# Reordering VectorE's work in a gated mix of two state-space layers: spectral products, the inverse transform, and scans in interleaved steps

## The chip, the cores and the metric

The kernel runs on one core of a Trainium2 chip, as one launch. The metric is the device time of one execution in microseconds (us). Times of the kernel before are the median of three runs; one further execution was taken with the hardware profiler on, and every row of a profile below comes from that one.

The core has five engines with a queue of instructions each. TensorE (PE in the profile, with its weight loads as PEld) multiplies matrices into PSUM; VectorE (DVE) and ScalarE (ACT) work element by element on SBUF and PSUM; GpSimd (POOL) and SyncE (SP) are used here almost only to issue DMAs. An engine works its queue in program order and stops at an instruction that waits for another engine or for a DMA. A DMA issued by POOL with an accumulate operation (a "gather" below) adds one SBUF tile to another without an engine's work.

## The reference

Shapes: L = 2048 positions, D = P = 1024 channels and states. Cut to what matters:

```python
g = sigmoid((x * gate_w).sum(-1, keepdims=True))
# a: S5, a complex diagonal state-space model
Lam_bar = exp(dt * Lam);  Bu = x @ (((Lam_bar - 1) / Lam)[:, None] * B).T
h[t] = Lam_bar * h[t - 1] + Bu[t]                 # over L
a = 2 * real(h @ C.T) + x * Dskip
# b: H3-like
kv = (sum of 4 shifted k * shift_k taps) * v
y  = irfft(rfft(kv, 2 * L) * rfft(ssm_k, 2 * L))[:L] + kv * ssm_D    # per channel
b  = x * y
out = g * a + (1 - g) * b                         # 1 x 2048 x 1024, bf16
```

## The kernel before, in words

**Who sets the order.** Every instruction of an engine goes through `put` (line 94), which chains it behind the last one of the same engine; so each engine's order is the order in which the program calls it, and the profile names line 94 for nearly everything. Groups have to be told apart by their tiles. Pieces of the work are written as generators; `step`, `steps(gen, n)` and `run` (lines 1078 to 1087) advance one by one, by n, or to its end, and this is how different pieces are woven together.

**The long convolution (first 163 us or so).** Eight chunks of 128 channels, c = 0 to 7. Positions are split by remainder modulo 4, so that the transform becomes matmuls with small cosine and sine tables, on even and odd parts. For each chunk:

- `taps` (571): the four shifted taps of k on TensorE, from tiles kT and kB, evacuated by ACT into `ks`.
- `times_v` (601): VectorE multiplies `ks` by v (row "ks<-ks,v"); then the generator yields; a `mirror` matmul on TensorE turns half of it round, ACT evacuates it into `lo`; yield; VectorE takes the odd part `ev` = ks − lo ("ev<-ks,lo"), and the even part is made by a gather ("ks<-lo", ks += lo), issued on POOL behind ev because it overwrites what ev reads.
- `fwd_K` (634) and `fwd_V` (672): the forward transforms of ssm_k and of kv, matmuls into psk and psv. ACT evacuates them to the spectra (a BT tile, and `Vh`). fwd_V reads ev and ks.
- `products` (685): the product of the two spectra as a 4 x 4 block convolution on VectorE, elementwise, into `acc` (the tile `sums`) with temporaries `wkh` (the tile `WK`) and `t`. Its multiplies `first(0)`, `second(0)`, `first(1)`, `second(1)` are 4096 and 3072 elements wide per partition, then n2 (4096 wide) and n3 (2048 wide) and the adds into acc. One of the adds is a gather ("acc<-wkh", 768 KB). Last, two butterfly steps write the result over `Vh` ("acc<-acc", "Vh<-acc").
- `inverse` (753): for each of two halves (par = 0, 1), eight matmuls of 512 columns from Vh into psz; ACT evacuates them into `cv`, and SP stores cv to a scratch in DRAM.

The loop over chunks (1147 to 1244) works three chunks at once: the inverse of chunk c − 1 (`back`), the products of chunk c (`prod`), and the taps and transforms of chunks c + 1 and c + 2 (`tv` is times_v of chunk c + 1). Lines 1184 to 1197 hold the order that the change touches: one step of back, the mirror of tv, three steps of prod, the rest of tv (ev and its gather), one more step of prod, and later the second half of back. The product of the last chunk runs in the block "fin" (1301 to 1330) without the gather.

**S5 (from there to the end, part of it woven into the chunks).** `Bu` multiplies x by B into tiles U ("both", "even", "odd" in the profile), split in even and odd positions. `scan` (927) works one of 16 pieces: 4 blocks of 512 positions by 4 groups of 256 states. On VectorE it rotates the complex input by a table TCS (A = TC·U, trn = TS·U, two adds), runs four `tensor_tensor_scan` with a real decay, rotates back (U = TC·A, trn = TS·A, two adds into Ve), keeps the last column (`WL`, from which `carry` makes the next block's start `init`), and scales Ve by lambda in two parts. ACT does that scaling in the scans listed in `scaled_by_act`, VectorE in the others. Three sums then add these into the odd positions `Uo`. For scaling on ACT the sums are put off (`put_off`) until the next scan's four scan instructions are through. The last scan works its two halves one after the other.

`advance(j)` (1418) weaves scan j with the first step of scan j + 1. Behind it run, by the list `plan`, the matmuls of further Bu tiles and of the output: `Cy` and `Cy_group` multiply U, O and V (the scans' states) by CT into psy, which ACT evacuates scaled by g. For an output row, `scale_b` (1037) scales the convolution's row by 1 - g and the skip row by g (tile `gd`) on ACT and adds the one to the other by a gather on POOL ("pbb<-gd", "row<-gd" for row 11); `product(k)` (1068) multiplies that by x on VectorE ("xr<-xr,pbb", "row<-row" for row 11, called in scan 12 through `between`); `combine` (1072) adds it to S5's row by another gather ("m<-xr"), and `store` writes it out. The last four output rows (1510 to 1555) run over all states at the end: `added` (on VectorE) or `scaled_added` (on ACT, then an add on VectorE), and the stores.

Of the kernel before, what the change touches and what calls it, by code (L numbers as in the profile page):

```python
# [9 lines left out]
ALU = mybir.AluOpType  # L10
# [10 lines left out]
def kernel(  # L21
# [39 lines left out]
    NTB = S // TB  # L61
# [30 lines left out]
    def put(eng, f, *a, **kw):  # L92
        with tc.issue_after(prev[eng]) if eng in prev else nullcontext():
            i = f(*a, **kw)  # L94
        prev[eng] = getattr(i, "ins", i)
# [4 lines left out]
    def bc(ap, shape):  # L100
        return ap.to_broadcast(shape)
# [3 lines left out]
    def tt(o, a, b, op):  # L105
        put("dve", V.tensor_tensor, out=o, in0=a, in1=b, op=op)
# [578 lines left out]
    def products(c, h=0, home=u4, by_dma=True):  # L685
# [5 lines left out]
        def mult(a, t):  # L691

            if len(t.shape) == 2:
                t = t.rearrange("p (k y) -> p k y", k=2)
            t = t.rearrange("p k (c b x) -> p k c b x", c=2, x=w)
            k_ = bc(K[:, :, a:a + 1], [128, 2, 8 - 2 * a, w])
            v_ = bc(Vt[:, :, 0:4 - a].rearrange("p c b x -> p c (b x)")[:, None], [128, 2, 2, (4 - a) * w])
            tt(t, k_, v_, ALU.mult)
            return t
# [29 lines left out]
            tt(A[:, :, :, 1:], A[:, :, :, 1:], n1, ALU.add)  # L729
        if c > 0:  # L730
            yield
        n2 = mult(2, WK[:, 3072:7168] if c > 0 else home([128, 8 * w], BF16, "t"))
        n3 = mult(3, home([128, 4 * w], BF16, "t"))
        yield
        tt(n2[:, :, :, 1:], n2[:, :, :, 1:], n3, ALU.add)
        tt(A[:, 1, :, 2:], A[:, 1, :, 2:], n2[:, 1], ALU.add)
        yield
        tt(A[:, 0, :, 2:], A[:, 0, :, 2:], n2[:, 0], ALU.add)
        yield
        tt(A[:, 1, 1], A[:, 0, 0], A[:, 1, 1], ALU.subtract)  # L740
        tt(A[:, 1, 0], A[:, 0, 1], A[:, 1, 0], ALU.add)
        if c == 0 and h == 0:
# [178 lines left out]
            gather(V_, Q)  # L921
            yield

    put_off = []
    scaled_by_act = (4, 12, 13, 14)

    def scan(tb, g, fin):


        last = tb == NTB - 1 and g == NG - 1  # L930
        Ve, Uo = Us[tb, g]
        A = wk.tile([128, 2, 2, HB], BF16, name="A")

        b = None
        for js in ([slice(0, 1), slice(1, 2)] if last else [slice(0, 2)]):
            g2 = slice(2 * g + js.start, 2 * g + js.stop)
            full = [128, 2, js.stop - js.start, HB]
            Aj, Uj = A[:, :, js], Ve[:, :, js]
            tt(Aj, bc(TC[:, g2][:, None], full), Uj, ALU.mult)
            if js.start == 0:  # L940
                yield
                b = wk.tile([128, 2, 2, HB], BF16, name="trn", bufs=1)
            bj = b[:, :, js]
            tt(bj, bc(TS[:, g2][:, None], full), Uj, ALU.mult)
            if js.start == 0:
                if g == 0 and tb > 0:
                    carry(tb)
                step(fin)
            tt(Aj[:, 0], Aj[:, 0], bj[:, 1], ALU.add)
            tt(Aj[:, 1], Aj[:, 1], bj[:, 0], ALU.subtract)  # L950
            for j in range(js.start, js.stop):
                pi = 2 * g + j
                for c in range(2):
                    put("dve", V.tensor_tensor_scan, out=A[:, c, j], data0=bc(rv2[:, pi:pi + 1], [128, HB]),
                        data1=A[:, c, j], initial=0.0 if tb == 0 else init[tb][:, c, pi:pi + 1],
                        op0=ALU.mult, op1=ALU.add)
            while put_off:
                put_off.pop()[1]()
            if js.start == 0:
                run(fin)  # L960
                hbs[tb, g] = Ve
            hb = hbs[tb, g][:, :, js]
            tt(hb, bc(TC[:, g2][:, None], full), Aj, ALU.mult)
            if tb < NTB - 1:
                copy(WL[tb][:, :, g2], Aj[:, :, :, HB - 1])
            tt(bj, bc(TS[:, g2][:, None], full), Aj, ALU.mult)
            if not last:
                yield
            tt(hb[:, 0], hb[:, 0], bj[:, 1], ALU.subtract)
            tt(hb[:, 1], hb[:, 1], bj[:, 0], ALU.add)  # L970
            by_act = tb * NG + g in scaled_by_act or last and js.start == 0
            if tb * NG + g == 3:
                run(turning[7])
                product(0)
            if by_act:
                q = [s5p["Q"].tile([128, 2, 2, HB], BF16, name="Q") for k in range(2)]
            else:
                q = A, b

            def scaled(q=q):  # L980
                for k in range(2):
                    for j in range(js.start, js.stop):
                        a = (q[k][:, :, j], hbs[tb, g][:, :, j], lam[:, k, 2 * g + j:2 * g + j + 1])
                        if by_act:
                            act(a[0], a[1], func=ACT.Identity, scale=a[2])
                        else:
                            ts(*a, None, ALU.mult)

            def summed(q=q, js=js):
                o, (q1, q2) = Uo[:, :, js], [x[:, :, js] for x in q]  # L990
                tt(o, o, q1, ALU.add)
                tt(o[:, 0], o[:, 0], q2[:, 1], ALU.subtract)
                tt(o[:, 1], o[:, 1], q2[:, 0], ALU.add)

            if last and js.start == 0:
                scaled()
                first_half = summed
            elif by_act:
                put_off.append((scaled, summed))
            else:  # L1000
                if last:
                    first_half()
                scaled()
                summed()

    ios, gas = {}, {}

# [70 lines left out]
    def step(gen):  # L1078
        next(gen, None)
# [67 lines left out]
    for c in range(NC - 1):  # L1147
# [38 lines left out]
        step(tabs)  # L1186
        if c == 6:
            step(parts)
        step(back)
        step(tv)  # L1190
        steps(prod, 3)
        run(tv)
        step(prod)
        step(old)
        step(tabs)
        run(back)
        run(old)
        fk = none
        if nn < NC:
# [245 lines left out]

    step(scans[0])
    for j in range(NS):
        for k in loaded.get(j, ()):
            loads(k)
# [107 lines left out]
```

## Time and profile before

| what | value |
|---|---|
| median of three runs | 382.99 us (382.91 to 383.02) |
| the profiled execution | 383.41 us |
| its span, first to last instruction | 381.6 us |
| mean granted TensorE clock | 0.997 |
| VectorE busy share of three 20-us stretches: 160 to 180, 220 to 240, 320 to 340 | 19.90, 19.66, 19.69 us of 20 |

A row of a timeline gives the start from the beginning of the span, the busy time, the engine, the line, the operation, the tiles (written <- read) with partitions x elements and type, and "xN" for N alike in a row, whose busy time is then from the first start to the last end. A bracket at the end is idle time of that engine ahead of the row and what ended it. An instruction's busy time is longer than the distance to the next start where the two overlap; so the cost of an instruction is read as the distance of starts. Rows of DMA issues give the KB of each and the median time from issue to landing. The sum of idle times of POOL counts for little, since it only issues.

### The profile page before, as it was taken

What the parts mean: (1) busy time and instruction counts of PE and PEld (TensorE: products, weight loads), DVE (VectorE), ACT (ScalarE), POOL (GpSimd) and SP (SyncE); (2) the same over time, 40 slices, a digit from 0 to 9 for tenths busy, and PEclk for the clock granted to TensorE, in tenths of its full rate; (3) what the DMA queues carried; (4) which work ended last, traced back from release to release, by engine and by line L of the source; (5) the groups of instructions that cost most, each with busy time, mean ns of one, the idle gap of its engine ahead of it and who ended that gap; (6) DMA issues with size and microseconds to landing.
All of it is one profiled execution on the core that took longest, in us unless ns stands there. A gap on an engine that the chain in (4) does not pass through costs nothing.

```text
span 381.6 us, 6664 instructions
## 1 busy us (share of the span) xinstructions
PE 374.0 (98%) x2469; PEld 201.0 (53%) x2469; DVE 370.8 (97%) x566; ACT 309.5 (81%) x475; POOL 80.3 (21%) x109
## 2 busy tenths in 40 slices
PE   8999999999999999999999999999999999999995
PEld 6656367574674846644454444444444444444434
DVE  8899999999999999999999999999999999999996
ACT  5879998988979998786949999986989669937621
POOL 4011030110301103041002113122415233635000
PEclk9999999999999999999999999999999999999998
DMA  7989999999999998959999999958798999998902
GB/s 167 167 113 260 221 208 185 225 210 223 202 171 197 214 203 188 180 126 154 210 208 209 218 196 210 241 127 143 152 236 162 235 249 229 166 246 142 221 1 110
DMA packets 126259, 71.78 MB, mean 188 GB/s; under 512 B 104649, under 2 KB 107601, under 8 KB 126226
## 3 DMA queue, kind: packets, MB, share of 16 engines
q1 hardware_dynamic: 112416, 45.90, 55.9%
q0 software_dynamic: 12688, 25.17, 39.2%
q8 instruction: 19, 0.31, 0.4%
q10 hardware_dynamic: 1122, 0.28, 0.4%
q14 instruction: 14, 0.11, 0.1%
HBM read 15.48 MB, written 8.39 MB: 63 GB/s over the span
## 4 chain that ended last, share of the span: by engine, by line
DVE 50%; PE 19%; issue 14%; DMA 9%; ACT 5%; POOL 2%; DVEq 0%; POOLq 0%; ACTq 0%
DVE acc L94 14%; DVE wkh L94 9%; PE both L94 9%; DVE A L94 7%; DMA U<-Q 5%; DVE U L94 4%; DMA row<-gd 3%; DVE t L94 3%; DVE trn L94 3%; DVE Vh L94 2%; PE taps L94 2%; PE psz L94 2%; DVE ks L94 2%; ACT Q L94 2%; PE psk L94 2%
## 5 line engine op out<-in xcount | busy, mean ns | idle before, releaser
L94 PE MATMUL psy<-CT,U 128*128 128x512 bf16 (+1 forms) x426 | 93.4, 374 | 0.9 <-DVE U L94 0.9
L94 PEld LDWEIGHTS <-U 128*128 128x128 bf16 x492 | 48.0, 98 | 56.9 <-DVE U L94 1.4
L94 PEld LDWEIGHTS <-BT 128*128 128x128 bf16 x544 | 50.5, 98 | 33.4
L94 ACT ACTIVATE Q<-U,lam 128x512 bf16<-128x512 bf16 (+1 forms) x66 | 39.0, 635 | 15.9 <-DVE U L94 15.9
L94 DVE TENSOR_TENSOR wkh<-BT,Vh 128x3072 bf16<-128x3072 bf16 (+3 forms) x24 | 44.2, 1842 | 0.2
L94 POOL DMA_DIRECT2D U<-Q x26 | 26.1, 1018 | 83.4 <-ACT Q L94 35.7
L94 DVE TENSOR_TENSOR acc<-BT,Vh 128x4096 bf16<-128x4096 bf16 (+3 forms) x19 | 36.9, 1949 | 0.3 <-ACT Vh L94 0.2
L94 PE MATMUL both<-xT,BT 128*128 128x512 bf16 x160 | 35.3, 379 | 0.0
L94 ACT ACTIVATE Vh<-psv 128x1024 bf16<-128x1024 f32 x32 | 30.7, 1032 | 5.5 <-PE psv L94 5.5
L94 ACT ACTIVATE BT<-psk 128x1024 bf16<-128x1024 f32 x31 | 30.3, 1032 | 3.3 <-PE psk L94 3.1
L94 DVE TENSOR_TENSOR acc<-acc,wkh 128x2048 bf16<-128x2048 bf16 (+3 forms) x23 | 32.3, 1431 | 0.5
L94 DVE TENSOR_TENSOR_SCAN A<-rv,init,A 128x256 bf16<-128x256 f32 x48 | 32.2, 731 | 0.0
L94 ACT ACTIVATE U<-both 128x512 bf16<-128x512 f32 x44 | 24.2, 594 | 9.6 <-PE both L94 9.3
L94 POOL DMA_DIRECT2D acc<-wkh x8 | 9.8, 1219 | 103.3 <-DVE wkh L94 103.3
L94 PE MATMUL psk<-eok,SF 128*128 128x384 bf16 (+1 forms) x120 | 28.5, 354 | 0.0
L94 PEld LDWEIGHTS <-SF 128*128 128x128 bf16 x184 | 18.0, 98 | 18.8
L94 PE MATMUL psz<-Vh,CI 128*128 128x512 bf16 x64 | 24.3, 380 | 0.0
L94 PE MATMUL psz<-Vh,SI 128*128 128x512 bf16 x64 | 24.3, 379 | 0.0
L94 PEld LDWEIGHTS <-kT 128*128 128x128 bf16 x352 | 22.2, 103 | 1.3 <-DMA kT<-in_B_k_dram 0.8
L94 PE MATMUL taps<-dg,kT 128*128 128x128 bf16 (+1 forms) x352 | 22.6, 216 | 0.0
L94 PE MATMUL both<-xT,BTl 128*128 128x512 bf16 x96 | 21.2, 379 | 0.0
L94 PE MATMUL both<-BT,BT 128*128 128x512 bf16 x96 | 21.0, 379 | 0.0
(223 smaller groups left out, 770.1 us busy)
## 6 DMA issues: line engine op xcount, KB each, us to landing
U<-Q POOLq DMA_DIRECT2D x26, 256.0 KB, 5.1
acc<-wkh POOLq DMA_DIRECT2D x6, 768.0 KB, 8.6
cv_scr<-cv SPq DMA_DIRECT2D x16, 256.0 KB, 7.5
kn<-in_B_ssm_k_dram SPq DMA_DIRECT2D x5, 512.0 KB, 4.8
v<-in_B_v_dram SPq DMA_DIRECT2D x5, 512.0 KB, 6.1
out_dram<-m SPq DMA_DIRECT2D x8, 256.0 KB, 4.4
BT<-cv_scr SPq DMA_DIRECT2D x7, 256.0 KB, 7.5
out_dram<-BT SPq DMA_DIRECT2D x7, 256.0 KB, 2.0
```

Source lines behind the costliest of these rows:

```text
L94: i = f(*a, **kw)
```

## The change

In **products** for the chunks behind the first: n3 is multiplied ahead of n2; n2's multiply is issued as two of half the width (k = 1, then k = 0), the add of n3 into n2 and the add of n2 into acc's first part as two halves each. In the **chunk loop** the inverse runs whole ahead of the mirror, and a fourth step of the products stands ahead of the rest of times_v. **Scans** are cut into four steps; `advance` takes three steps of scan j + 1 in turn with those of scan j; the temporary trn has two buffers; the three sums of scan j are handed on in `to_add` and issued between the four scan instructions of scan j + 1; of what ACT scales only the scaling is put off. The last scan's order is written out by hand, with the first rotation at full width and its first half scaled by VectorE too.

In the diff the old body of scan, which stands above in full, is left out at "...".

```diff
--- before.py
+++ after.py
@@ -729,14 +729,28 @@
             tt(A[:, :, :, 1:], A[:, :, :, 1:], n1, ALU.add)
         if c > 0:
             yield
-        n2 = mult(2, WK[:, 3072:7168] if c > 0 else home([128, 8 * w], BF16, "t"))
-        n3 = mult(3, home([128, 4 * w], BF16, "t"))
-        yield
-        tt(n2[:, :, :, 1:], n2[:, :, :, 1:], n3, ALU.add)
-        tt(A[:, 1, :, 2:], A[:, 1, :, 2:], n2[:, 1], ALU.add)
-        yield
-        tt(A[:, 0, :, 2:], A[:, 0, :, 2:], n2[:, 0], ALU.add)
-        yield
+        if c > 0:
+            n3 = mult(3, home([128, 4 * w], BF16, "t"))
+            n2 = WK[:, 3072:7168].rearrange("p (k c b x) -> p k c b x", k=2, c=2, b=2)
+            for k in (1, 0):
+                tt(n2[:, k], bc(K[:, k:k + 1, 2:3], [128, 2, 2, w]), Vt[:, :, 0:2], ALU.mult)
+            yield
+            for k in (1, 0):
+                tt(n2[:, k, :, 1:], n2[:, k, :, 1:], n3[:, k], ALU.add)
+            tt(A[:, 1, :, 2:], A[:, 1, :, 2:], n2[:, 1], ALU.add)
+            yield
+            for i in (0, 1):
+                tt(A[:, 0, i, 2:], A[:, 0, i, 2:], n2[:, 0, i], ALU.add)
+            yield
+        else:
+            n2 = mult(2, home([128, 8 * w], BF16, "t"))
+            n3 = mult(3, home([128, 4 * w], BF16, "t"))
+            yield
+            tt(n2[:, :, :, 1:], n2[:, :, :, 1:], n3, ALU.add)
+            tt(A[:, 1, :, 2:], A[:, 1, :, 2:], n2[:, 1], ALU.add)
+            yield
+            tt(A[:, 0, :, 2:], A[:, 0, :, 2:], n2[:, 0], ALU.add)
+            yield
         tt(A[:, 1, 1], A[:, 0, 0], A[:, 1, 1], ALU.subtract)
         tt(A[:, 1, 0], A[:, 0, 1], A[:, 1, 0], ALU.add)
         if c == 0 and h == 0:
@@ -921,87 +935,112 @@
             gather(V_, Q)
             yield
...
+    put_off, to_add = [], []
     scaled_by_act = (4, 12, 13, 14)
     def scan(tb, g, fin):
         last = tb == NTB - 1 and g == NG - 1
+        by_act = tb * NG + g in scaled_by_act
         Ve, Uo = Us[tb, g]
+        g2 = slice(2 * g, 2 * g + 2)
+        halves = [slice(0, 1), slice(1, 2)] if last else [slice(0, 2)]
+        def wide(t, js):
+            return bc(t[:, 2 * g + js.start:2 * g + js.stop][:, None], [128, 2, js.stop - js.start, HB])
         A = wk.tile([128, 2, 2, HB], BF16, name="A")
...
+        tt(A, wide(TC, slice(0, 2)), Ve, ALU.mult)
+        yield
+        b = wk.tile([128, 2, 2, HB], BF16, name="trn")
+        tt(b, wide(TS, slice(0, 2)), Ve, ALU.mult)
+        if g == 0 and tb > 0:
+            carry(tb)
+        yield
+        tt(A[:, 0], A[:, 0], b[:, 1], ALU.add)
+        tt(A[:, 1], A[:, 1], b[:, 0], ALU.subtract)
+        yield
+        def scan_of(c, j):
+            pi = 2 * g + j
+            put("dve", V.tensor_tensor_scan, out=A[:, c, j], data0=bc(rv2[:, pi:pi + 1], [128, HB]),
+                data1=A[:, c, j], initial=0.0 if tb == 0 else init[tb][:, c, pi:pi + 1],
+                op0=ALU.mult, op1=ALU.add)
+        def turned_back(js):
+            tt(Ve[:, :, js], wide(TC, js), A[:, :, js], ALU.mult)
+            if tb < NTB - 1:
+                copy(WL[tb][:, :, g2], A[:, :, :, HB - 1])
+            tt(b[:, :, js], wide(TS, js), A[:, :, js], ALU.mult)
+        def joined(js):
+            tt(Ve[:, 0, js], Ve[:, 0, js], b[:, 1, js], ALU.subtract)
+            tt(Ve[:, 1, js], Ve[:, 1, js], b[:, 0, js], ALU.add)
+        q = A, b
+        if by_act:
+            q = [s5p["Q"].tile([128, 2, 2, HB], BF16, name="Q") for k in range(2)]
+        def scaled(js=slice(0, 2)):
+            for k in range(2):
+                for j in range(js.start, js.stop):
+                    a = (q[k][:, :, j], Ve[:, :, j], lam[:, k, 2 * g + j:2 * g + j + 1])
+                    if by_act:
+                        act(a[0], a[1], func=ACT.Identity, scale=a[2])
+                    else:
+                        ts(*a, None, ALU.mult)
+        def sums(js=slice(0, 2)):
+            o, (q1, q2) = Uo[:, :, js], [x[:, :, js] for x in q]
+            return [lambda: tt(o, o, q1, ALU.add),
+                    lambda: tt(o[:, 0], o[:, 0], q2[:, 1], ALU.subtract),
+                    lambda: tt(o[:, 1], o[:, 1], q2[:, 0], ALU.add)]
+        hbs[tb, g] = Ve
+        before = list(to_add)
+        to_add.clear()
+        step(fin)
+        if not last:
+            for j in range(2):
                 for c in range(2):
...
+                    scan_of(c, j)
+                    if before and (c, j) != (0, 0):
+                        before.pop(0)()
+            run(fin)
+            yield
+            turned_back(halves[0])
+            yield
+            joined(halves[0])
+            yield
             if tb * NG + g == 3:
                 run(turning[7])
                 product(0)
             if by_act:
...
+                put_off.append(scaled)
             else:
...
                 scaled()
+            to_add.extend(sums())
+            return
+        run(fin)
+        j0, j1 = halves
+        scan_of(0, 0)
+        scan_of(1, 0)
+        before.pop(0)()
+        turned_back(j0)
+        scan_of(0, 1)
+        joined(j0)
+        scan_of(1, 1)
+        scaled(j0)
+        before.pop(0)()
+        turned_back(j1)
+        before.pop(0)()
+        joined(j1)
+        for f in sums(j0):
+            f()
+        scaled(j1)
+        for f in sums(j1):
+            f()
     ios, gas = {}, {}
@@ -1186,14 +1225,12 @@
         step(tabs)
         if c == 6:
             step(parts)
-        step(back)
+        run(back)
         step(tv)
-        steps(prod, 3)
+        steps(prod, 4)
         run(tv)
-        step(prod)
         step(old)
         step(tabs)
-        run(back)
         run(old)
         fk = none
         if nn < NC:
@@ -1417,9 +1454,10 @@
 
     def advance(j):
         step(scans[j])
-        if j + 1 < NS:
-            step(scans[j + 1])
-        run(scans[j])
+        for k in range(3):
+            if j + 1 < NS:
+                step(scans[j + 1])
+            step(scans[j])
 
     def Cy_row(k):
         loads(k + 3)
@@ -1439,11 +1477,12 @@
             Cy_g(tb, tl, [ps[:, 0], ps[:, 1]], g, g == NG - 1)
             if g == NG - 1:
                 if tb == 2 and tl == 0:
-                    put_off[-1][0]()
+                    put_off.pop()()
                 scale_a(k, [(slice(0, D), flat(ps))])
                 combine(k)
 
-    step(scans[0])
+    for k in range(3):
+        step(scans[0])
     for j in range(NS):
         for k in loaded.get(j, ()):
             loads(k)
@@ -1469,7 +1508,7 @@
                 scale_b(k)
             run(turn)
         if j == 4:
-            put_off[-1][0]()
+            put_off.pop()()
             scale_b(3)
         for unit in plan[j].split():
             if unit == "C0":
@@ -1478,8 +1517,8 @@
                 Cy_group(int(unit[1]), int(unit[2]))
             else:
                 (Bu_next if unit[0] == "B" else Cy_row)(int(unit[1:]))
-        if put_off and j not in (4, 12):
-            put_off[-1][0]()
+        if put_off:
+            put_off.pop()()
         if j == 10:
             step(turn)
             for k in scaled_b[j]:
```

More of the change, by code (lines that the diff above doesn't have):

```diff
@@ L922, in turn_U @@
             yield
-    put_off = []
+    put_off, to_add = [], []
     scaled_by_act = (4, 12, 13, 14)
@@ L930, in scan @@
         last = tb == NTB - 1 and g == NG - 1
+        by_act = tb * NG + g in scaled_by_act
         Ve, Uo = Us[tb, g]
+        g2 = slice(2 * g, 2 * g + 2)
+        halves = [slice(0, 1), slice(1, 2)] if last else [slice(0, 2)]
+        def wide(t, js):
+            return bc(t[:, 2 * g + js.start:2 * g + js.stop][:, None], [128, 2, js.stop - js.start, HB])
         A = wk.tile([128, 2, 2, HB], BF16, name="A")
[L934 to L952, printed above, removed]
-                for c in range(2):
[L954 to L971, printed above, removed]
@@ L975, in scan @@
             if by_act:
-                q = [s5p["Q"].tile([128, 2, 2, HB], BF16, name="Q") for k in range(2)]
+                put_off.append(scaled)
             else:
[L978 to L995, printed above, removed]
-                scaled()
[L997 to L1004, printed above, removed]
+                scaled()
+            to_add.extend(sums())
[19 more added lines that the diff above has]
+            f()
     ios, gas = {}, {}
```

## The prediction

> **What bounds the kernel now.** I read the page first: busy shares and the chain of waits.
>
> ```profile
> span 381.6 us, 6664 instructions
> PE 374.0 (98%) x2469; PEld 201.0 (53%) x2469; DVE 370.8 (97%) x566; ACT 309.5 (81%) x475; POOL 80.3 (21%) x109
> DVE 50%; PE 19%; issue 14%; DMA 9%; ACT 5%; POOL 2%; DVEq 0%; POOLq 0%; ACTq 0%
> ```
>
> TensorE (PE) and VectorE (DVE) are both full, and the chain names VectorE. The chain follows semaphores, and says nothing of how much would be left if that engine were faster. So I asked for busy time by stretch (PE, PEld, DVE, ACT, POOL with their instruction groups, PEclk, DMA share, GB/s), and for the long waits:
>
> ```profile
> 220.00:240.00 20.00, 20.00 (x95) 9.08 (x93) 19.66 (x40) 19.85 (x29) 4.34 (x6) 1.00 1.11 205
> ...
> PE mirror L94 <- DVE ks L94: 1.5, 4, 0.4
> PEld L94 <- DVE Vh L94: 1.2, 3, 0.5
> ```
>
> In this stretch of the scan stage PE issues 95 matmuls in 20 us, one per 0.21 us, with granted clock 1.00. That is a PE without a gap; VectorE can only gain there what PE loses by waiting. PE loses in three places, which its timeline prices:
>
> ```profile
> 139.00 0.38 PE L94 MATMUL psz<-Vh,SI 128*128 128x512 bf16 x1
> 139.75 0.60 PE L94 MATMUL mirror<-ks,refl 128*128 128x512 bf16 x2 [0.37 <-DVE ks L94]
> ...
> 116.18 0.38 PE L94 MATMUL psz<-Vh,SI 128*128 128x512 bf16 x1
> 116.57 0.61 PE L94 MATMUL mirror<-ks,refl 128*128 128x512 bf16 x2
> ...
> 90.51 0.59 PE L94 MATMUL psv<-ks,SF 128*128 128x512 bf16 x2
> 91.11 0.39 PE L94 MATMUL psz<-Vh,CI 128*128 128x512 bf16 x1
> ...
> 360.76 7.07 PE L94 MATMUL psy<-CT,U 128*128 128x512 bf16 x32
> 368.74 5.35 PE L94 MATMUL psy<-CT,U 128*128 128x512 bf16 x24 [0.91 <-DVE U L94]
> ```
>
> (a) The mirror waits for ks: 0.75 from start to start at 139.00, against 0.216 for neighbours that do not wait (32 matmuls from 360.76 take 31 such steps and 0.38), so 0.53 is lost; 0.39 − 0.216 = 0.17 at 116.18. The waits row has four of the large kind; with two of the small kind that is 4 × 0.53 + 2 × 0.17 ≈ 2.46 us. (b) psz waits for Vh, three times; at 90.51 it loses 0.60 − 0.43 = 0.17, and about 0.4 us in all three. (c) psy waits for U once: 368.74 − 360.76 − 32 × 0.216 = 1.07 us. More than 2.46 + 0.4 + 1.07 ≈ 3.9 us PE cannot give back, whatever VectorE saves.
>
> **What a dependent neighbour costs.** A chunk and a scan on VectorE's timeline:
>
> ```profile
> 122.50 0.68 DVE L94 TENSOR_TENSOR ev<-ks,lo 128x1024 bf16<-128x1024 bf16 x1
> 123.10 1.75 DVE L94 TENSOR_TENSOR wkh<-BT,Vh 128x3072 bf16<-128x3072 bf16 x1
> 124.89 1.76 DVE L94 TENSOR_TENSOR acc<-acc,wkh 128x3072 bf16<-128x3072 bf16 x1
> 126.68 2.29 DVE L94 TENSOR_TENSOR wkh<-BT,Vh 128x4096 bf16<-128x4096 bf16 x1
> 128.89 1.22 DVE L94 TENSOR_TENSOR t<-BT,Vh 128x2048 bf16<-128x2048 bf16 x1
> 130.14 1.23 DVE L94 TENSOR_TENSOR wkh<-wkh,t 128x2048 bf16<-128x2048 bf16 x1
> 131.40 2.36 DVE L94 TENSOR_TENSOR acc<-acc,wkh 128x2048 bf16<-128x2048 bf16 x2
> ...
> 138.47 1.22 DVE L94 TENSOR_TENSOR ks<-ks,v 128x2048 bf16<-128x2048 bf16 x1
> 139.61 2.29 DVE L94 TENSOR_TENSOR acc<-BT,Vh 128x4096 bf16<-128x4096 bf16 x1
> ...
> 301.57 0.69 DVE L94 TENSOR_TENSOR A<-TCS,U 128x1024 bf16<-128x1024 bf16 x1
> 302.17 0.75 DVE L94 TENSOR_TENSOR U<-U,trn 128x512 bf16<-128x512 bf16 x2
> ...
> 304.01 0.69 DVE L94 TENSOR_TENSOR U<-U,A 128x1024 bf16<-128x1024 bf16 x1
> 304.73 0.76 DVE L94 TENSOR_TENSOR U<-U,trn 128x512 bf16<-128x512 bf16 x2
> ```
>
> A successor that does not need its predecessor starts before it ends: 0.60 after a 1024-wide one (122.50, 301.57), 1.14 after 2048 (138.47). One that does starts after its end: 0.72 after 1024 (304.01 to 304.73), 1.25 after 2048 (128.89 to 130.14), 1.79 instead of 1.67 after 3072. So each dependence costs 0.12 us of VectorE, at every width.
>
> **The change part by part.**
>
> *Products.* Chunk c = 4 has six dependent starts (124.89, 126.68, 130.14, 131.40, and one inside or ahead of each of the two pairs behind it); the new order keeps one: 5 × 0.12 = 0.59 saved. It adds three instructions: one 4096-wide multiply (2.21, 126.68 to 128.89) becomes two of 1.14, +0.08; two 2048-wide adds become two of 0.60 each, 2 × 0.06. Net −0.39 per chunk, −0.27 in the chunk where eok already stands between two of them. Up to the last product that a psz waits for, four such chunks and that one: 4 × 0.39 + 0.27 = 1.83 us earlier.
>
> *Inverse whole ahead of the mirror.* PE executes the second eight psz matmuls, 8 × 0.216 = 1.73 us, before it asks for ks, which is at most 0.53 late: loss (a) goes. What is late next is Vh, loss (b), since PE now comes to psz earlier. So the chunk stage gains the smaller of PE's losses, 2.46, and what VectorE allows: 1.83 up to the last Vh plus the 0.53 of the mirror behind it, 2.36. I take **2.3**; the bounds are 1.83 and 2.46 + 0.4. The second cv evacuation and its store come earlier past the mirror's evacuation lo: ACT works cv, cv, lo. SP's and GpSimd's queues keep their order. lo ends about two matmul groups later, and ev, behind it, is not wanted so soon (next).
>
> *ev moves behind a multiply.* ev now follows the second 3072-wide product, 123.10 to 124.89 less the dependence: 1.67 later. The gather ks<-lo waits for ev, and psv for the gather:
>
> ```profile
> 120.68 1.20 POOL L94 DMA_DIRECT2D acc<-wkh  x1 [17.28 <-DVE wkh L94]
> 123.48 0.90 POOL L94 DMA_DIRECT2D ks<-lo  x1 [1.61 <-DVE ev L94]
> ...
> acc<-wkh POOLq DMA_DIRECT2D x6, 768.0 KB, 8.6
> ks<-lo POOLq DMA_DIRECT2D x6, 256.0 KB, 7.1
> ...
> 134.39 0.59 PE L94 MATMUL psv<-ks,SF 128*128 128x512 bf16 x2
> ```
>
> Issued at 123.48, it lands some 7 to 9 us later, at 132.5 at the latest by the queue ahead of it (120.68 + 8.6 = 129.3 for three times its bytes, and a third of 8.6 more): 1.9 us before 134.39. If the queue sets the landing, 1.67 costs nothing; if the issue does, 0.2 us are left here, and less in chunks whose psv comes sooner. I take nothing, since acc<-wkh is still in flight when ks<-lo is issued either way.
>
> *Scans interleaved.* Some 60 dependences go in 16 scans, about 0.6 us of VectorE in a middle one. PE does not wait for VectorE there, so VectorE only runs ahead, until an input stops it: product(11), "row<-row", whose gather is the last of seven in a burst.
>
> ```profile
> 324.47 0.86 POOL L94 DMA_DIRECT2D V<-Q  x1 [6.09 <-ACT Q L94]
> ...
> 327.77 11.58 DMA row<-gd
> ...
> 338.59 2.67 DVE L94 TENSOR_TENSOR_SCAN A<-rv,init,A 128x256 bf16<-128x256 f32 x4
> 341.18 0.67 DVE L94 TENSOR_TENSOR row<-row 128x1024 bf16<-128x1024 bf16 x1
> ...
> 362.33 1.53 DVE L94 TENSOR_TENSOR U<-U,Q 128x1024 bf16<-128x1024 bf16 x3
> ```
>
> It lands at 327.77 + 11.58 = 339.35, and follows ACT and so PE's evacuations: with PE 2.3 earlier I take 337.05, P = 337.1 for the product (it was 341.18). The new order puts scan 14's sums, now done at 362.33 + 1.53 = 363.86, between pieces of scan 15. Laid out with 0.60 for a 1024-wide step, 0.34 for 512 (302.17, a pair in 0.75), about 0.21 for 256, 0.27 for a scaling (estimates), and (341.18 − 338.59)/4 = 0.65 for a scan instruction: product 0.60; the turns of two scans at 4 × 0.60 + 4 × 0.34, with four scan instructions and sums of 0.60 + 2 × 0.34, 7.64 each; to the next scan instruction 3.76; then two of them 1.30, a sum 0.60, half a turn back 0.68 + 0.41, two more 1.30, two scalings 0.54, a sum 0.34, two multiplies 0.68 and the second sum 0.34, together 6.19. They end at P + 25.8 = 362.9. PE wants them in the group of 32 behind 360.76, at its nineteenth matmul, 360.76 + 18 × 0.216 = 364.65, or 362.35 when 2.3 earlier. So loss (c), 1.07, gives way to a wait of 0.55: **0.5** gained. Bounds: nothing lost (1.07) if the row lands earlier, and the rivals below. Scan 15's own parts, laid out the same way with its first half scaled on VectorE instead of ACT, come before PE's use.
>
> *The tail.*
>
> ```profile
> 376.55 1.04 PE L94 MATMUL psy<-CT,U 128*128 128x256 bf16 x8
> ...
> 377.31 0.42 DVE L94 TENSOR_TENSOR BT<-BT,xlast 128x512 bf16<-128x512 bf16 x1
> 377.65 0.87 DVE L94 SCALAR_TENSOR_TENSOR BT<-psy,gcols,xlast 128x256 bf16<-128x256 f32 x2
> ```
>
> PE ends at 377.59, VectorE at 378.52, with one 256-wide piece (0.43) still queued when PE is done. VectorE with its scans done earlier has no such backlog: **0.4**, between 0 and 0.43.
>
> **Sum.** 2.3 + 0.5 + 0.4 = 3.2 us. The profiled execution took 383.41 (span 381.6), 0.42 above the median 382.99 of runs from 382.91 to 383.02; so 380.2 for such an execution, **379.8** as a median. Own range 379.0 to 380.8.
>
> **The rivals.**
>
> *The gather lands with its issue.* ks<-lo 1.67 later in each chunk; the chunk with the least slack makes PE wait 1.4 to 1.9. Of the 2.3 about 0.95 stays: 381.2. For it: 7.1 us for 256 KB is hardly less than 8.6 for 768 KB, so the time isn't bytes alone.
>
> *The row gather does not follow PE.* Landing at 339.35, P = 339.4, the sums end at 365.2, PE waits 2.85 instead of 1.07: 383.41 − 2.3 − 0.4 + 1.78 − 0.42 = 382.1. For it: seven transfers in one queue, 324.47 to 339.35, 2.1 us each.
>
> *The product comes later than now (slower).* VectorE now stands at a product inside scan 12 and everything behind it is one unbroken chain, 3.1 us longer up to scan 14's sums than before (25.8 against 363.86 − 341.18 = 22.7). Each us that P is late is then one us at the end. It breaks even where PE's wait is 1.07 + 2.7 = 3.77: P = 340.3. One transfer of 2.1 us more ahead of the row, on a landing that does not move, gives 341.5 and 382.99 + 1.2 = 384.2. Against it: GpSimd's queue order is unchanged.
>
> *The order gains nothing (slower).* If every VectorE successor waited for its predecessor's end, there would only be the 21 added instructions, 7 × 0.20 = 1.4, on Vh and PE's psz; scan 14's sums would come some 3 us later than PE wants them: 1.4 + 2.7 gives 387. Against it stand the two start distances, 0.60 and 0.72. The Trainium skill ("VectorE: DVE Perf Modes", section "The DRAIN you can't avoid") says that the next operation doesn't start until the pipe is empty, and that leaving out semaphores does not change it; this trace has 1024-wide operations of 0.69 whose successors start 0.60 later, and does not agree.
>
> *VectorE is the bound.* If PE's full rows hid idle time, all of 92 × 0.12 − 1.4 = 9.6 us would show: 373.4. Against it: 0.216 per matmul in every stretch without a wait. The Trainium skill ("Perfetto Trace Analysis", section "Identifying the Most-Contended Engine") advises to judge TensorE by its weight loads, not by matmul busy time; here these are 53%, and by that reading PE has room. The start distances decide against it.
>
> **How the numbers follow.** Forecast 0.50, gather with its issue 0.13, row not following 0.12, product late 0.15, order without effect 0.05, VectorE bound 0.03, others 0.02. A measurement tells from no change what exceeds 0.2%, 0.77 us: below 382.22 is faster. Faster: 0.50 + 0.13 + 0.03 and half of the row case, 0.72. Same: its other half, a little of the late product, 0.09. Slower 0.19. The range: from all of PE's losses and the tail gone (3.9 + 0.4, and a little: 378.3) to 383.0, which takes in the row case and the cheap end of a late product; 0.8 lies inside.
>
> **What would show it.** On VectorE's timeline of a chunk one dependent start is left, and the chunk's period falls only as far as PE's does. No mirror waits for ks; psz waits for Vh by a tenth or two. psv<-ks must not wait for a DMA (the first rival). The row product starts near 337, with idle time ahead of it; psy waits once more, for about half a us, near 362. The forecast fails if P is above 340.3, if psv waits for ks<-lo, or if independent starts are not 0.60 in the new order.

## The result, and the profile after

| | before | after |
|---|---|---|
| median of 15 runs each | 383.08 us | 381.04 us |
| from, to (four executions left out) | 382.79 to 383.31 | 379.36 to 384.79 |
| profiled execution, span | 383.41, 381.6 us | 381.04, 379.3 us |

The ratio is 0.9946 with a 95% interval of 0.993 to 0.9962: 2.0 us faster. The forecast was 379.8 in a range of 378.3 to 383.0. What it did not foresee is the second row: the kernel before repeats within half a microsecond here, the changed one spreads over several. (Beside the experiments below, the kernel before had executions of 384.2 us and more too, 7 of 30 in one round; most of its executions stay within a microsecond.) Four executions, three of the kernel before (389.0 to 398.15 us) and one of the changed one (391.86), ran in a slower state of the core and are left out of the second row and of the ratio.

The page of the changed kernel, its busy shares and its chain of waits:

```profile
span 379.3 us, 6647 instructions
PE 369.9 (98%) x2434; PEld 200.3 (53%) x2469; DVE 364.1 (96%) x585; ACT 307.6 (81%) x473; POOL 79.1 (21%) x109
DVE 55%; PE 26%; issue 8%; DMA 5%; ACT 4%; POOL 0%; SPq 0%; POOLq 0%; DVEq 0%
```

VectorE is busy 6.7 us less. The shares of the chain hide where it runs; its pieces in order of time (start, us, what) do not. From 307 us to the end it is TensorE alone:

```profile
307.39 10.74 PE psy L94 x49
...
372.14 3.67 PE psy L94 x32
375.81 0.03 issue
375.84 0.48 DVE BT L94
```

Before, the same stretch of the chain was VectorE's scans, from the row's gather at 327.77 on. The engine that ends the kernel has changed.

The chunk that answers to the one shown of before, on VectorE:

```profile
121.08 1.75 DVE L94 TENSOR_TENSOR wkh<-BT,Vh 128x3072 bf16<-128x3072 bf16 x1
122.75 0.68 DVE L94 TENSOR_TENSOR ev<-ks,lo 128x1024 bf16<-128x1024 bf16 x1
123.35 1.75 DVE L94 TENSOR_TENSOR acc<-acc,wkh 128x3072 bf16<-128x3072 bf16 x1
125.02 1.21 DVE L94 TENSOR_TENSOR t<-BT,Vh 128x2048 bf16<-128x2048 bf16 x1
126.15 2.35 DVE L94 TENSOR_TENSOR wkh<-BT,Vh 128x2048 bf16<-128x2048 bf16 x2
128.43 1.28 DVE L94 TENSOR_TENSOR wkh<-wkh,t 128x1024 bf16<-128x1024 bf16 x2
129.63 2.42 DVE L94 TENSOR_TENSOR acc<-acc,wkh 128x2048 bf16<-128x2048 bf16 x3
...
136.63 1.22 DVE L94 TENSOR_TENSOR ks<-ks,v 128x2048 bf16<-128x2048 bf16 x1
137.77 2.28 DVE L94 TENSOR_TENSOR acc<-BT,Vh 128x4096 bf16<-128x4096 bf16 x1
```

The add behind ev starts 0.60 after it, the multiply t 1.67 behind the 3072-wide add (it was 1.79 for a dependent one). From ev to the next ks multiply it is 13.88 us, where before it was 15.97; 1.67 of that is the multiply that now stands ahead of ev, the other 0.42 is what a chunk saves (forecast 0.39).

TensorE at the mirror, at the first psv of chunk 6, at its first psy, and at the end:

```profile
139.38 0.38 PE L94 MATMUL psz<-Vh,SI 128*128 128x512 bf16 x1
139.59 0.59 PE L94 MATMUL mirror<-ks,refl 128*128 128x512 bf16 x2
...
152.13 0.38 PE L94 MATMUL psv<-ev,CF 128*128 128x512 bf16 x1
152.89 0.59 PE L94 MATMUL psv<-ks,SF 128*128 128x512 bf16 x2 [0.37 <-DMA ks<-lo]
...
250.32 1.02 PE L94 MATMUL psy<-CTa,U 128*128 128x512 bf16 x4 [1.51 <-ACT U L94]
...
360.05 12.03 PE L94 MATMUL psy<-CT,U 128*128 128x512 bf16 x54
```

The mirror follows psz after 0.21: loss (a) is gone. So is the wait for U near 367, loss (c): 54 matmuls run through. Two waits are new, both on a transfer in the end: psv for ks<-lo, and the first psy, which waits for PSUM that ACT has not emptied. ACT is late because of this row (before, then after):

```profile
213.10 0.22 ACT L94 ACTIVATE U<-ends 128x4 bf16<-128x4 bf16 x1 [0.74 <-DMA U<-Q]
```

```profile
212.57 0.22 ACT L94 ACTIVATE U<-ends 128x4 bf16<-128x4 bf16 x1 [2.51 <-DMA U<-Q]
```

The copy writes the tile of the eighth Bu pair, whose buffer the tile Q had; Q is free when the second of two chained gathers U<-Q has landed. ACT came 2.3 us earlier to this place. The first of the two gathers was issued 2.3 us earlier as well (202.25, then 199.95), but the two took 4.5 and 5.7 us to land before and take 5.6 and 6.5 now, so the second lands only half a microsecond earlier. ACT has no gap afterwards up to 249 us. That is where 1.6 of TensorE's 2.3 us went.

The product that was to pin VectorE, and the tail:

```profile
334.05 0.40 DVE L94 TENSOR_TENSOR U<-U,trn 128x512 bf16<-128x512 bf16 x1
337.52 0.69 DVE L94 TENSOR_TENSOR row<-row 128x1024 bf16<-128x1024 bf16 x1 [3.07 <-issue]
...
362.84 0.42 DVE L94 TENSOR_TENSOR U<-U,Q 128x512 bf16<-128x512 bf16 x1
...
374.63 0.48 DVE L94 SCALAR_TENSOR_TENSOR BT<-psy,gcols,xlast 128x256 bf16<-128x256 f32 x1
375.84 0.48 DVE L94 SCALAR_TENSOR_TENSOR BT<-psy,gcols,xlast 128x256 bf16<-128x256 f32 x1 [0.72 <-PE psy L94]
```

VectorE stands still for 3.07 us ahead of the product, until the row's gather lands (issued at 325.55, 11.9 us to landing); it starts at 337.52 (forecast 337.1), and scan 14's last sum starts at 362.84 and ends at 363.26, 25.7 behind it (forecast 25.8). The last add waits for TensorE, where before it waited in VectorE's own queue.

### The profile page after: what moved, and what is told of

Its sections match the earlier page's. It is cut to its first block, busy times and chain, and to the rows that moved or that the text cites. A ratio compares the mean times of both kernels' runs of the same rounds, so it can differ in the third digit from the quotient of the medians.

```text
span 379.3 us, 6647 instructions
## 1 busy us (share of the span) xinstructions
PE 369.9 (98%) x2434; PEld 200.3 (53%) x2469; DVE 364.1 (96%) x585; ACT 307.6 (81%) x473; POOL 79.1 (21%) x109
## 4 chain that ended last, share of the span: by engine, by line
DVE 55%; PE 26%; issue 8%; DMA 5%; ACT 4%; POOL 0%; SPq 0%; POOLq 0%; DVEq 0%
PE psy L94 23%; DVE acc L94 20%; DVE wkh L94 13%; DVE A L94 5%; DVE Vh L94 4%; DVE t L94 3%; DVE U L94 2%; DVE ks L94 2%; DMA U<-Q 2%; ACT Q L94 2%; DVE trn L94 2%; PE taps L94 1%; DMA kT<-in_B_k_dram 1%; DMA BT<-gd 1%; DVE CT L94 1%
## 5 line engine op out<-in xcount | busy, mean ns | idle before, releaser
L94 DVE TENSOR_TENSOR wkh<-BT,Vh 128x2048 bf16<-128x2048 bf16 (+3 forms) x31 | 44.6, 1457 | 0.0
L94 ACT ACTIVATE Q<-U,lam 128x512 bf16<-128x512 bf16 (+1 forms) x64 | 37.5, 632 | 8.5 <-DVE U L94 8.5
L94 DVE TENSOR_TENSOR_SCAN A<-rv,init,A 128x256 bf16<-128x256 f32 x48 | 34.4, 738 | 0.0
L94 DVE TENSOR_TENSOR acc<-acc,wkh 128x1024 bf16<-128x1024 bf16 (+4 forms) x30 | 32.7, 1128 | 0.1
L94 PE MATMUL taps<-dg,kT 128*128 128x128 bf16 (+1 forms) x352 | 21.5, 208 | 1.0 <-DMA kT<-in_B_k_dram 1.0
L94 PEld LDWEIGHTS <-kT 128*128 128x128 bf16 x352 | 20.8, 99 | 2.5 <-DMA kT<-in_B_k_dram 2.0
L94 DVE TENSOR_TENSOR U<-U,trn 128x512 bf16<-128x512 bf16 (+1 forms) x58 | 21.2, 391 | 0.1
```

## The experiments

Two theories of the gain that was lost and of the spread. **Landing**: TensorE, no longer held back by VectorE, meets transfers whose landing doesn't move with it and differs from run to run. **Scans**: the new waits come from the interleaved order of the scans. Runs of one round of experiments share a chip and the runs of the kernel before.

**e0_after and e8_after: the change itself, again.** No edit.

> The changed kernel once more, for its own spread. Theory (landing): the chunk stage's gain of 2.3 us on TensorE meets a transfer that does not come earlier: ACT, at the copy 'U<-ends' near 212 us, waits for the tile that the second of two chained gathers U<-Q still reads, 2.51 us instead of 0.74, and TensorE later waits 1.67 us for PSUM that ACT has not yet emptied. As transfers land a us or two earlier or later from run to run, the median is 381.0 and runs spread over 379.4 to 382.5. Rival (scans): the wait comes from the interleaved scans; then it is the same in every profile, and the spread has another cause.

> The changed kernel as a control beside the three below, on the same chip. Median 380.9, runs from 378.6 to 382.6.

Measured 380.75 (378.59 to 382.64, ratio 0.9931, 0.9904 to 0.9958) and 380.24 (379.47 to 382.53). The profiled execution of e0 took 378.77 us, 2.3 less than the first one. Its TensorE has no wait for ks<-lo, and none at the first psy:

```profile
246.63 1.46 PE L94 MATMUL both<-BT,BT 128*128 128x512 bf16 x6
248.03 1.02 PE L94 MATMUL psy<-CTa,U 128*128 128x512 bf16 x4
```

The same program, so the waits are not in the order of its instructions alone. The three profiles bear the landing theory out: they differ in these waits (and e8 in one more, for kT, in the table below), and about as much in time. The two gathers U<-Q, from the first issue to the second landing, took 12.6 us in the first profile, 9.5 in e0 and 11.2 in e8.

**e1_chunks and e2_scans: one half of the change each.** e1 has the hunks of products and of the chunk loop alone, e2 all others.

> Products and chunk loop as changed, scans as before. Landing: TensorE is 2.3 us earlier at 170 us, ACT waits some 2.5 us for U<-Q near 212, TensorE some 1.5 us before its first psy near 250, about 0.7 us is left behind that, and the wait for U near 367 stays at 1.07 or less: 382.0 (381.5 to 382.5). Rival (scans): no longer wait near 212, TensorE 2.3 us earlier all the way to 360 us, where the old scans make it wait 1.1 to 3: 380.7 to 382.0.

> Scans as changed, products and chunk loop as before. Landing: TensorE as before up to 360 us, ACT's wait near 213 stays at 0.7, the wait of 1.07 for U near 367 is gone and the tail is 0.4 shorter: 381.6. Rival (scans): ACT's wait near 213 and a wait of over 1 us before the first psy near 250 appear here too: 383.0.

e1: 380.55 (380.15 to 381.16), ratio 0.9929 (0.9908 to 0.9949), better than I had expected. e2: 382.26, ratio 0.9967 (0.9947 to 0.9988). The rows that decide are these, of e1 (the last from its chain of waits) and of e2:

```profile
154.31 0.59 PE L94 MATMUL psv<-ks,SF 128*128 128x512 bf16 x2 [1.74 <-DMA ks<-lo]
...
250.14 1.02 PE L94 MATMUL psy<-CTa,U 128*128 128x512 bf16 x4
...
375.65 0.48 DVE L94 SCALAR_TENSOR_TENSOR BT<-psy,gcols,xlast 128x256 bf16<-128x256 f32 x1 [0.36 <-PE psy L94]
...
292.52 83.11 PE psy L94 x400
```

```profile
251.54 1.02 PE L94 MATMUL psy<-CTa,U 128*128 128x512 bf16 x4 [0.64 <-ACT U L94]
```

In e1's profile TensorE loses 1.74 us for a transfer, and the execution is still 2 us faster than before. My forecast of 382.0 had TensorE wait at the first psy and near 367, and it waits at neither: VectorE's chain through the old scans is 2.84 us earlier (row "U<-U,Q", 362.33 to 359.49), so the 1.07 us that TensorE had lost there are gained. Behind 154.31 TensorE runs without a wait and ends this execution, but hardly: VectorE's last piece waits 0.36 us for it, so without the 1.74 us VectorE would have set an end only some 0.4 us earlier, an estimate from that row. With VectorE's chain so near, waits of TensorE show little in the time; that fits the narrow range of e1, and it may be why the kernel before, whose end VectorE sets, mostly repeats so well. e2 has a wait at the first psy with TensorE only 0.2 us earlier than before; e1, without the new scans, has none there. One profile of each can't tell whether the scans make that wait likelier, and e5 below has it without them.

**e5_inverse and e6_products: the chunk loop's order alone, the products' order alone.**

```diff
-        step(back)
+        run(back)
         step(tv)
-        steps(prod, 3)
+        steps(prod, 4)
         run(tv)
-        step(prod)
...
-        run(back)
```

e6 is the diff's first hunk (products) alone.

> Only the chunk loop's order changed (inverse whole, mirror and ev later), products and scans as before. By the prediction TensorE no longer waits for the mirror, but for Vh, since VectorE is no faster: the losses move to psz, about 0.5 us is gained by the mirror of the last chunk, nothing at the end, where VectorE's chain sets the time: 382.8 (382.4 to 383.1). If the mirror's waits themselves were the loss: 380.5.

> Only the products' order changed, loop and scans as before. VectorE's period falls by 0.39 where nothing else holds it, TensorE still waits for ks in each chunk, less by what VectorE gains. By the prediction VectorE comes 2.0 to 2.5 us earlier behind the chunks, and as its chain sets the end, the time falls by about as much as TensorE allows, 1.5 to 2.4: 381.0. If dependences cost nothing in this order (21 more instructions only): 383.7.

e5: 382.89 against 383.16, ratio 0.9994 (0.9985 to 1.0003), no change. e6: 381.03, ratio 0.9944 (0.9932 to 0.9957). Both as expected. In e5's profile (383.92, the longest of its twelve executions) the mirror's waits are gone and TensorE waits for Vh, 0.56 us for ks<-lo, and at the first psy instead; some of its waits, with what they waited for:

```profile
ACT U L94 <- DMA U<-Q: 3.3, 1, 3.3
...
PEld L94 <- DVE Vh L94: 2.5, 5, 0.9
...
PE psy L94 <- ACT U L94: 1.7, 1, 1.7
```

And the wait for U<-Q, 3.3 us, is there with the old scans and the old products: the interleaved scans are not what causes it, and the scans theory falls. e6, with the old scans too, has the same two waits, and VectorE ends it without waiting for TensorE:

```profile
212.97 0.22 ACT L94 ACTIVATE U<-ends 128x4 bf16<-128x4 bf16 x1 [1.91 <-DMA U<-Q]
...
250.72 1.02 PE L94 MATMUL psy<-CTa,U 128*128 128x512 bf16 x4 [0.91 <-ACT U L94]
...
375.78 0.94 DVE L94 SCALAR_TENSOR_TENSOR BT<-psy,gcols,xlast 128x256 bf16<-128x256 f32 x2
```

Taking away dependences on VectorE is worth 2.1 us by itself; the new place of the inverse nothing by itself. The products' order alone (0.9944) is thus as fast as the whole change was in the result (0.9946); the changed kernel beside the experiments was at 0.9931 and 0.9929, with intervals that overlap e6's. That the other two parts add anything to it is not shown.

**e4_ev_back and e11_ev_back: ev at its old place, in the changed kernel.**

```diff
-        steps(prod, 4)
+        steps(prod, 3)
         run(tv)
+        step(prod)
```

> The changed kernel with ev at its old place, ahead of the second 3072-wide multiply, so that ks<-lo is issued 1.67 us earlier. If the issue sets the landing (the prediction's rival): TensorE never waits for ks<-lo, and runs lose what they lose there, 0.3 to 1.9 us, median 380.2. If the queue sets it, behind acc<-wkh: landing near 152 as with the change, the median stays at 380.9 (0.12 us of VectorE for one dependence per chunk is added).

> The kernel of e4 again (ev ahead of the second 3072-wide multiply), since its profile was of a disturbed run and its median, 379.75, had no changed kernel beside it. If the issue of ks<-lo matters, it stays below the control by 0.5 to 1.2 us; if only the queue matters, it is within 0.3 of the control.

e4 gave 379.75 (0.9903, 0.9886 to 0.992), with no changed kernel beside it. With one, e11 gave 380.87 (380.32 without its two longest, 387.02 and 388.49) against 380.24 of e8: no gain. The view of the tile ks around chunk 6's gather says why; first the changed kernel (e0), then e11 (duration of the issue, when it was issued, time to landing):

```profile
L94 POOL DMA_DIRECT2D ks<-lo x1: 896/896/896, 146.1 to 146.1; - x1
DMA to landing us min/median/max: 5.9/5.9/5.9
```

```profile
L94 POOL DMA_DIRECT2D ks<-lo x1: 896/896/896, 145.2 to 145.2; - x1
DMA to landing us min/median/max: 7.8/7.8/7.8
```

Issued 0.9 earlier, it landed a us later. In e9, issued at 144.8, it took 8.9; in e1, issued at 146.3, 8.0; in e7, issued at 146.1, 6.2. Landings between 152.0 and 154.3 with no order in them by issue: the prediction's rival "lands with its issue" falls, and nothing here speaks against its assumption that ev's new place costs nothing. What the wait comes from is that TensorE asks for ks at about 152 to 152.5 instead of 154.45; before the change this gather was issued at 146.7 and landed at 153.7, in time by 0.75 us.

**e3_inverse7 and e7_u8: two ways round ACT's wait.** e3 moves the last inverse ahead of the eighth Bu pair, to give ACT work; e7 gives that pair's U a buffer of its own.

```diff
+        back = inverse(c)
+        step(back)
+        run(back)
         b10, b11 = Bu(8)
         run(b10)
         run(b11)
-    back = inverse(c)
-    step(back)
-    run(back)
```

```diff
-            if i in (6, 7, 8, 15):
+            if i == 8:
+                U = s5p["u8"].tile(shape, BF16, name="U8")
+            elif i in (6, 7, 15):
...
     m_pool = pool("m", 2, side="right")
+    s5p["u8"] = pool("u8", 1, side="right")
...
-        prod, back = products(c, 0, room, False), inverse(c - 1)
+        prod, back = products(c, 0, u4, False), inverse(c - 1)
```

> The changed kernel with the inverse of the last chunk ahead of the eighth Bu pair, so that ACT evacuates cv (1.93 us) while the gather is still under way. Landing: ACT's work behind the wait is 1.9 us less, TensorE's wait before the first psy shrinks from 1.67 to 0.2 or less, median 379.5, with a narrower spread. Rival (scans): the wait is not by the gather's landing, ACT loses as much somewhere else: 381.0.

> The changed kernel with a tile of its own for the eighth Bu pair's U (and n3 of the last product in the pool that this leaves free), so that ACT's copy 'U<-ends' near 212 us need not wait for the gather that still reads Q. Landing theory: ACT's wait there is gone, TensorE's wait before the first psy is 0.1, as in the fastest profile of the change (378.77); median 379.6, and what spread is left comes from ks<-lo. If the wait near 250 us has another cause, it stays: 380.9.

e3 was slower, 386.1 (ratio 1.0093, 1.0059 to 1.0127): the last product isn't done there, and TensorE waits for Vh, so that this run decides nothing between the theories (its profile, 389.71, is of the longest of its seven executions):

```profile
207.47 0.59 PE L94 MATMUL psz<-Vh,CI 128*128 128x512 bf16 x1 [4.23 <-DVE Vh L94]
207.84 0.63 PE L94 MATMUL psz<-Vh,SI 128*128 128x512 bf16 x1
208.27 0.63 PE L94 MATMUL psz<-Vh,CI 128*128 128x512 bf16 x1
```

e7 gave 379.39 (ratio 0.9904, 0.9885 to 0.9923). In its profile ACT does not wait, and TensorE comes to the first psy without a gap:

```profile
209.46 0.20 ACT L94 ACTIVATE U<-ends 128x4 bf16<-128x4 bf16 x1
```

```profile
248.21 1.02 PE L94 MATMUL psy<-CTa,U 128*128 128x512 bf16 x4
```

e9 and e10, with the same buffer, have no wait there either. Such a profile alone proves little, as e0 and e1 have none with the shared buffer. But where the buffer is shared the two waits go together: ACT's waits of 2.51, 1.91, 1.64 and 1.14 us for U<-Q (first profile, e6, e2, e8) are followed by waits of TensorE at the first psy of 1.51, 0.91, 0.64 and 0.15, a microsecond less each time, and ACT's waits of 0.93 or less (e11, the kernel before, e1) by none. (e5's 3.35 us are followed by two waits of TensorE for ACT, 0.5 and 1.67.) So the chain from the buffer's release to the first psy is shown, and with it why ACT's 0.74 us before the change cost nothing.

**e9_both and e10_both_old_scans.** e9 is e7 and e4 together; e10 the same with the old scans.

> The changed kernel with both: U of the eighth pair in a tile of its own, and ev at its old place. Landing theory: TensorE has next to no wait left but for the start and Vh, in every run: median 378.8, spread under 1 us. If the two waits are not what separates the change from 378.6: 379.4 or more, spread as with e7.

> The kernel of e9 with the scans of before. VectorE's chain through the scans is then 2.5 to 2.9 us earlier than before the change, no more, and ends the kernel: 380.3, with a narrow spread. The difference to e9, some 1.4 us, is what the interleaved scans are worth once TensorE does not wait for transfers. If the scans bring nothing, both are the same.

e9: 380.41, e10: 381.29, the changed kernel beside them 380.24. e9 misses: its executions spread from 379.40 to 384.94 where I had expected less than a microsecond; its profile has no wait at the first psy, but psv waits 1.50 us for ks<-lo, the largest of the changed scans' kernels. So removing one of the waits is not shown to make the kernel faster than the change, and no kernel here is shown to beat it. The scans are worth 0.6 us alone (e2), some 0.9 here (e10 against e9, whose intervals overlap: 0.9941 to 0.9976 and 0.9902 to 0.9967) and nothing beside e1 (380.55 against 380.75 of e0).

What the waits are worth shows when six profiles with the changed scans and products stand side by side (e3 is left out, which loses its time at Vh, and e4, whose profile is of its longest execution, 386.61). Of the table's waits, each is a row like those above or a row of the waits view, whose lines for e8 are these:

```profile
PE taps L94 <- DMA kT<-kT: 0.9, 1, 0.9
```

```profile
249.50 1.02 PE L94 MATMUL psy<-CTa,U 128*128 128x512 bf16 x4 [0.15 <-ACT U L94]
```

| kernel | psv for ks<-lo | first psy | taps for kT<-kT | sum | profiled execution |
|---|---|---|---|---|---|
| e0_after | 0 | 0 | 0 | 0 | 378.77 |
| e7_u8 | 0.23 | 0 | 0 | 0.2 | 378.92 |
| e11_ev_back | 0.46 | 0 | 0 | 0.5 | 379.68 |
| e8_after | 0 | 0.15 | 0.9 | 1.05 | 380.23 |
| e9_both | 1.50 | 0 | 0 | 1.5 | 380.30 |
| after | 0.37 | 1.51 | 0 | 1.9 | 381.04 |

The order of the sums is the order of the times, at 378.7 to 379.2 plus the sum (waits for the first loads, in the first 11 us, are left out; they differ by up to half a microsecond). The first profile, whose 381.04 us are the median too, is thus a kernel of about 379 with some two microseconds of transfers that TensorE waits for, now at one place, now at another. That the executions without a profile, up to 384.79, differ for the same reason is likely, but not shown.

## Why the prediction was right or wrong

It was right in sign and its range holds the time; it was 1.2 us too low, and two errors in it partly cancel, which is luck.

- *Dependent neighbours, 0.12 each.* Right. A chunk saves 0.42 (0.39). VectorE is 2.1 us earlier at chunk 5's first butterfly, 157.46 to 155.33, 0.17 of it from the start; so 1.95 for the 1.83 of the sum. The rival without effect falls, with e6's 2.1 us. For that rival the prediction names the Trainium skill ("VectorE: DVE Perf Modes", section "The DRAIN you can't avoid") and finds that the trace does not agree; the same paragraph goes on to say that a next operation which is not held starts earlier, and with that the 0.60 agrees.
- *Inverse ahead of the mirror, 2.3.* TensorE was 2.30 earlier behind the chunks in the first profile, as forecast, and about 3.0 in e0, of which 0.6 come from the first loads (its first psk at 11.56 instead of 12.16), ahead of anything that was changed. But the step that the prediction built it on, that VectorE can only gain what TensorE loses by waiting, was only half of it: e5 takes the mirror's waits away and gains nothing, e6 leaves more than half of them (1.4 of 2.46 us) and gains 2.1. Before the change VectorE's chain ended the kernel, and TensorE's wait of 1.07 us at the end was the room in which its other waits vanished.
- *ev later, at nothing.* An earlier issue brought no earlier landing, so the price of the move holds; the place was wrong: I priced it in one chunk, which has 1.9 us to spare, and chunk 6 had 0.75. There psv waits, because TensorE comes earlier, 0 to 1.7 us by the profile. In the first profile that is 0.37 us, one of the three signs by which the prediction said that it would fail.
- *The wait for U, 1.07 to 0.55.* P was 337.52, the sums came where forecast, and TensorE, later than I had put it, did not wait at all: 1.07 gained. The landing was met, but not by the reason given, that the row follows TensorE: its burst of gathers went out 2.2 us earlier (324.47 to 322.26) with TensorE only 0.7 earlier at that time, and in e2 2.15 earlier with TensorE 0.5 later. In e0 the row came earlier still, P was 334.29, and TensorE did not wait although it was 3.0 earlier.
- *The tail, 0.4.* TensorE ended at 375.80 and VectorE at 376.32, 0.52 later instead of 0.93: 0.41.
- *The step that failed* is the sentence that TensorE without its three losses is 2.3 us earlier up to 360 us. The transfers were asked about only at ks<-lo and at the row; the release of a buffer by U<-Q near 212 us, where ACT already waited 0.74 us before, was not looked at. It took 1.6 us in the first profile. The rival in which a landing does not follow TensorE was right as a mechanism, at another transfer, and with a landing that differs from one execution to the next instead of staying where it was.
- In sum, for the first profile: 2.3 − 1.6 + 1.07 + 0.41, and 0.1 of rounding and of the start, is 2.3 of span. For e0 it is 3.0 + 1.07 + 0.4, which is nearly all of the 4.6 us by which it is faster. The forecast's gain of 3.2 was short by some 1.3, of which 0.6 are the first loads and 0.55 the wait for U that did not come; the waits for transfers, about 2 us in the first profile, it had at nothing.

## What to carry to other kernels

Where two engines are both full, ask which one ends the kernel: waits of the other are free until the room at the end is used up, and become time when the first gets faster. Before reckoning with a gain on the engine that takes over, list each place where it or its helpers already wait for a transfer or for a buffer that a transfer releases, however short the wait is now, and take the gain off there. Where the runs of a kernel spread after a change, look for waits on transfers in its path: several profiles of the same kernel show which.

## What the runs showed of the hardware

Gathers of one size differ in time to landing, at the same place of the same program: 5.9 to 6.9 us for chunk 6's ks<-lo in the three profiles of the changed kernel (8.0 in e1), and 9.5 to 12.6 us for the two chained gathers U<-Q, which is more than the change was worth. And in two profiles TensorE ran at about half its rate behind a long wait. Behind the 4.23 us in e3, matmuls of 512 columns start 0.43 us apart instead of 0.216; the granted clock by stretch of that kernel (the column behind POOL's):

```profile
200.00:205.00 5.00, 3.24 (x16) 1.27 (x13) 5.00 (x8) 4.94 (x11) 0.76 (x2) 1.00 1.10 228
205.00:210.00 5.00, 2.53 (x7) 0.92 (x8) 4.83 (x6) 4.35 (x5) 1.43 (x3) 0.61 1.23 239
210.00:215.00 5.00, 5.00 (x18) 2.02 (x17) 5.00 (x11) 2.15 (x3) 0.53 (x1) 0.71 1.04 208
215.00:220.00 5.00, 5.00 (x25) 2.25 (x23) 5.00 (x13) 1.09 (x2) 0.00 (x0) 1.00 0.93 226
```

In e10 the clock falls to 0.53 in the 3 us that begin some 2 us behind a wait of 2.59 us:

```profile
150.90 0.22 PE L94 MATMUL taps<-dg,kT 128*128 128x64 bf16 x2 [2.59 <-DMA kT<-kT]
153.19 3.19 PE L94 MATMUL even<-xT,BT 128*128 128x256 bf16 x16
```

```profile
153.00:156.00 3.00, 3.00 (x23) 2.24 (x21) 3.00 (x5) 1.33 (x4) 0.00 (x0) 0.53 0.96 196
```

Behind the 1.5 us of the first profile it stayed at 1.00. The Trainium skill ("TensorE: Matmul & The Clock Gate", section "Part 1: The HAM clock gate (the "warmup" mystery)") states a clock that is halved after an idle window of about 3.4 us, free-running, and restored after a busy one; the 4.23 us of e3 agree with it, while the wait in e10, 2.59 us, is shorter than that window. That the wait is what slowed the clock in e10 rests on one profile.
